# Cluster attention and a gated FFT convolution on one core: the last batch's products may run on GpSimd, two x1 blocks go through ScalarE, and the whole order is new

## The chip, the cores and the metric

The kernel runs on one core of a Trainium2 chip. The metric is device time in microseconds: the median of the runs of one program. A core has TensorE (PE, matmul), VectorE (DVE), ScalarE (ACT), GpSimd (POOL) and SyncE (SP, which issues DMAs here). Each engine takes its instructions in program order, so an instruction that waits holds up everything behind it on its engine.

## The reference

Inputs are q, k and v of shape 4 x 8 x 768 x 64 and 16 centroids per head. Each query and each key is given the nearest centroid of its head by cosine; a query attends only to keys with the same centroid:

```python
q_assign = np.argmax(np.einsum('bhsd,hcd->bhsc', q_n, c_n), axis=-1)
k_assign = np.argmax(np.einsum('bhsd,hcd->bhsc', k_n, c_n), axis=-1)
mask = q_assign[:, :, :, None] == k_assign[:, :, None, :]
scores = np.where(mask, scale * np.matmul(q, k.transpose(0, 1, 3, 2)), -1000000000.0)
attn = softmax(scores);  x = matmul(attn, v)          # heads joined: 4 x 768 x 512
```

The result x feeds a gated convolution along the sequence:

```python
proj = x @ w_proj;  x1, x2, x3 = proj[..., :D], proj[..., D:2*D], proj[..., 2*D:]
x2_conv = np.fft.irfft(np.fft.rfft(x2, axis=1) * np.fft.rfft(filter_fft, axis=0), axis=1)
out = (x1 * x2_conv * x3) @ w_out
```

## The kernel before, in words

The work is a list of small operations that a planner inside the kernel sets in order. For every operation there is an engine or a choice of engines with a cost for each, a due time, the data it reads and writes, and the PSUM banks it takes and gives back. The planner gives every engine the operation that can start first, and among nearly equal ones the one that is due first. `NUDGE` is a table that moves the due time of each numbered operation, and `ONLY` is a table that ties an operation to one engine. What comes out is one fixed order for each engine. The order is not decided on the chip.

There are eight groups of four heads (two groups make one batch), each in two halves of two heads. For a half, the scores are made in 18 PSUM banks (lines 82 and 84: scores, two 64-column matmuls for each product, or one of 128 columns), ScalarE takes the exponentials (L694, L697), TensorE multiplies by v (L708), and VectorE adds up the exponentials for the denominators (L725, L729). The routing of the next group lies between: transposes of q and k (L594, L607), copies into `qkP` and casts into `aug` (L282 on ScalarE, L284 on VectorE or GpSimd, one helper), similarities (L512, L627), the largest of each (L529 to L536, L638 to L642), masks (`ohT`, L653, L655) and DMAs of them into `aug`.

When two groups are done, the function `hyena(b)` does the convolution of their batch. It is spread over the attention of the next batch, except for the last batch, where nothing else is left to lie beside it. Its steps are these:

- U (L843): x2 in six PSUM banks. For the last batch, the part of four of them that needs the last heads (`kt` = 3) is a matmul of its own. Sums and differences follow (L857, L862) into `uv2`.
- The spectrum (L84, L475), its products with the filter's spectrum (L873, VectorE, two for each of six banks), and their sums into `y` (L877, VectorE or GpSimd).
- G, 16 banks (L84 on `xT`, `wpj`): for each of four blocks of 128 channels (`dt`) and each half of the sequence (`ch`), x3 and x1. x3 is copied out (L282 or L284); then VectorE multiplies x1, straight from PSUM, into that copy (L917, the gate). In the last batch the copies lie in `qkP`, which the routing no longer needs.
- The inverse transform, two banks for each `dt` (L84 or L82 on `inv`, `y`). One is copied to `od` (or `rb`), sum and difference go into `sd` (L944) for `dt` 0 and 1, and a fold makes the values in their order, in `yy` for even `dt` and `sim` for odd (L954). For `dt` 2 and 3 of the last batch the fold reads PSUM itself.
- The product with the gate into `y2` (L959): in the last batch two of 384 columns for each `dt`, on VectorE.
- W (L84 on `wout`, `y2`): six blocks of 128 rows of the output, copied out of PSUM and written by DMA (L982, L1001, L1005).

VectorE and GpSimd operations that are marked `lock` get an order between them: a GpSimd one waits until the last such VectorE one that stands before it in the program is done.

For x1 before the change (line 916):

```python
                    else:
                        op(("DVE", .55), lambda e, ch=ch, x3=x3, h=h: T.nc.vector.tensor_tensor(
                            x3()[:, ch], ap(h)[:, :384], x3()[:, ch], op=Alu.mult), due + .8,
                           r=[h], w=xkeys[ch], free=[h])
```

Of the kernel before, what the change touches and what calls it, by code (L numbers as in the profile page):

```python
# [19 lines left out]
Alu = mybir.AluOpType  # L20
# [66 lines left out]
class Plan:  # L87
# [6 lines left out]
    def op(self, eng, fn, due, r=(), w=(), alloc=None, free=(), lock=False, byts=0, after=(), kind=None, lat=0.0, tab=None):  # L94
        o = Op()
        o.eng = eng if isinstance(eng, dict) else {eng[0]: eng[1]}
        o.fn, o.due, o.alloc, o.free, o.lock, o.byts, o.kind = fn, due, alloc, free, lock, byts, kind
        o.seq = len(self.ops)
        o.due += NUDGE.get(o.seq, 0.0)
        o.outs, o.end, o.start, o.on = [], None, None, None  # L100
        deps, o.soft = set(after), set(after)
        o.lat, o.tab = lat, tab
        for key in r:
            deps.update(self.writers.get(key, ()))
        for key in w:
            deps.update(self.writers.get(key, ()))
            deps.update(self.reads.get(key, ()))
        for key in r:
            self.reads.setdefault(key, []).append(o)
        for key in w:  # L110
            self.writers[key] = [o]
            self.reads[key] = []
        deps.discard(o)
        o.deps = deps
        o.left = len(deps)
        for d in deps:
            d.outs.append(o)
        for h in free:
            h.readers += 1
        self.ops.append(o)  # L120
        return o
# [143 lines left out]
def build(T):  # L265

    P = Plan()
    op = P.op
# [11 lines left out]
    def copy(e, out, in_):  # L280
        if e == "ACT":
            T.nc.scalar.copy(out, in_)  # L282
        else:
            (T.nc.vector if e == "DVE" else T.nc.gpsimd).tensor_copy(out, in_)  # L284
# [3 lines left out]
    def ap(h):  # L288
        return bank(h.ids[0])
# [16 lines left out]
    def alu(e):  # L306
        return T.nc.vector if e == "DVE" else T.nc.gpsimd

    EV384 = {"ACT": .465, "DVE": .55}
# [507 lines left out]
    def hyena(b):  # L817
        xs = b % 2
        last = b == B - 1
# [12 lines left out]
        for m in range(3):  # L832
            pair_ = ((2, 3), (5, 4), (0, 1))[m]
            tb = m % 2
            for w_ in range(2):
                h = Bank()
                due = step(.87)
# [21 lines left out]
            if m == 2:  # L859
                for e_ in range(2):  # L860
                    for g_, o_ in ((0, Alu.add), (1, Alu.subtract)):
                        op({"DVE": .68, "POOL": 1.5}, lambda e, e_=e_, g_=g_, o_=o_: alu(e).tensor_tensor(  # L862
                            T.uv2[:, e_, g_], T.tm[0][:, 1 - e_], T.tm[1][:, 1 - e_], op=o_), due + 1.4 + .1 * e_,
                           r=[("tm", x, 1 - e_) for x in range(2)] + [("tm", x) for x in range(2)], w=[("uv2", e_, g_)], lock=True)
        for i in range(3):
            for cs in range(2):
                h = Bank()
                due = step(.44)
                op(("PE", .432), lambda e, i=i, cs=cs, h=h: spectrum4(ap(h), i, cs), due,
                   r=[("uv2", e_, m) for e_ in ((i,) if i < 2 else (0, 1)) for m in (e_ ^ cs, 2)] + [("fw", m, cs) for m in range(2)],  # L870
                   w=[h], alloc=h, kind="proj" if i < 2 else "half")
# [4 lines left out]
            for r in range(2):  # L876
                op({"POOL": 1.5, "DVE": .68}, lambda e, i=i, r=r: alu(e).tensor_tensor(  # L877
                    T.y[:, i, r], T.tm[r][:, 0], T.tm[r][:, 1], op=Alu.add if r else Alu.subtract), due + 2, r=[("tm", r, 0), ("tm", r, 1)],
                   w=[("y", i, r)], lock=True)
# [4 lines left out]
        for dt in range(ND):  # L884
# [13 lines left out]
            for ch in range(2):  # L898
                for off in (2 * DM, 0):
                    h = Bank()  # L900
                    due = step(.66)
                    if last:
                        due = w1 - 8 + 5 * ch + dt

                    def G(e, dt=dt, ch=ch, off=off, h=h):
                        for kt in range(ND):
                            x = T.xT[xs][:, kt, ts(ch, 384)].rearrange("p (t n) -> p t n", n=128)
                            columns(ap(h)[:, :384].rearrange("p (t n) -> p t n", n=128), T.wpj[:, kt, off + dt * 128:off + dt * 128 + 128],
                                    x[:, :, ::-1] if ch else x, kt == 0, kt == ND - 1)
                    g = op(("PE", .648), G, due, r=XT + WPJ, w=[h], alloc=h, kind="proj",  # L910
                           after=[] if last else gs[-1:] + (inv[dt - 2:dt - 1] if dt > 1 else []))
                    gs.append(g)
                    if off:
                        op(EV384, lambda e, ch=ch, x3=x3, h=h: copy(e, x3()[:, ch], ap(h)[:, :384]), due + .8,
                           r=[h], w=xkeys[ch], free=[h])
                    else:
                        op(("DVE", .55), lambda e, ch=ch, x3=x3, h=h: T.nc.vector.tensor_tensor(  # L917
                            x3()[:, ch], ap(h)[:, :384], x3()[:, ch], op=Alu.mult), due + .8,
                           r=[h], w=xkeys[ch], free=[h])
# [37 lines left out]
            for ch in range(2) if last else [slice(0, 2)]:  # L957
                cols = slice(384 * ch, 384 * ch + 384) if last else slice(0, S)
                op(("DVE", .55) if last else {"DVE": .95, "POOL": 2.1}, lambda e, dt=dt, ch=ch, cols=cols, x3=x3, yy=yy: alu(e).tensor_tensor(  # L959
                    T.y2[:, dt, cols], yy().rearrange("p t c -> p (t c)")[:, cols],  # L960
                    x3()[:, ch] if last else x3().rearrange("p a b -> p (a b)"), op=Alu.mult), due + 2.5,
                   r=ykeys[ch::2] + xkeys[ch] if last else ykeys + xkeys[0] + xkeys[1],
                   w=[("y2", dt, ch)] if last else [("y2", dt, 0), ("y2", dt, 1)], lock=True)
# [320 lines left out]
```

## Time and profile before

| what | value |
|---|---|
| runs | 372.38, 370.62, 372.59 us; median 372.38 us |
| the profiled execution's own time | 370.64 us |
| its span, first to last instruction | 368.9 us |
| TensorE busy | 357.5 us, 97% of the span |
| VectorE busy | 342.5 us, 93% |
| ScalarE busy | 263.6 us, 71% |
| GpSimd busy | 120.9 us, 33% |
| HBM traffic over the span | 106 GB/s on average |
| granted TensorE clock | 1.00 |

Busy time of an engine is the time in which one of its instructions runs. The chain that ended last is followed back from the last instruction, at each step to what released it. A group's row gives the line, the engine, what is written and read, the number of instructions, their busy time together and the mean time of one in ns; instructions of one engine overlap a little, so busy time can be less than number times mean.

### The profile page before, as it was taken

The page shows a single profiled execution, that of the slowest core. Times are in us where ns is not written, and L with a number is a line of the kernel's source. Part 1 is how long each engine was busy: PE and PEld are TensorE (multiplying, and loading weights), DVE is VectorE, ACT ScalarE, POOL GpSimd, SP SyncE. Part 2 cuts the span into 40 slices and gives each one's busy share as a digit, 9 for nine tenths or more (in the row PEclk, how much of TensorE's full clock was granted, in tenths as well). Part 3 has the DMA queues.
Part 4 walks back from the last instruction along what each step waited for, and adds up shares of the span by engine and source line. Part 5 has one row for each costly group of instructions (what it writes and reads, how often), then busy time and mean ns, then how long its engine had stood idle before and what let it go on. Part 6 is the DMA issues. An engine that isn't in the chain of part 4 may idle for free.

```text
span 368.9 us, 8653 instructions
## 1 busy us (share of the span) xinstructions
PE 357.5 (97%) x3314; PEld 208.9 (57%) x3316; DVE 342.5 (93%) x478; ACT 263.6 (71%) x495; POOL 120.9 (33%) x162
## 2 busy tenths in 40 slices
PE   7899999999999999999999999999999999999985
PEld 4455544555856565565555555566555655566672
DVE  7999999896999899999999999998998999999994
ACT  7998978877986859769869765899584785433242
POOL 7730730422032752331530044352221334016610
PEclk9999999999999999999999999999999999999999
DMA  7986597484247768748556964667477750110124
GB/s 175 202 189 126 128 211 195 93 189 110 62 80 156 115 156 169 152 103 129 107 64 183 238 170 81 146 152 98 81 116 167 150 77 1 48 45 2 59 115 171
DMA packets 90405, 46.20 MB, mean 125 GB/s; under 512 B 78248, under 2 KB 84092, under 8 KB 90364
## 3 DMA queue, kind: packets, MB, share of 16 engines
q1 hardware_dynamic: 85500, 36.15, 40.5%
q0 software_dynamic: 2752, 8.98, 17.1%
q10 hardware_dynamic: 2112, 0.52, 0.6%
q8 instruction: 26, 0.43, 0.5%
q14 instruction: 15, 0.12, 0.1%
HBM read 31.59 MB, written 7.40 MB: 106 GB/s over the span
## 4 chain that ended last, share of the span: by engine, by line
PE 78%; DVE 11%; ACT 5%; issue 3%; DMA 1%; POOL 1%; SPq 0%; DVEq 0%; ACTq 0%; POOLq 0%
PE bank L84 33%; PE pair L708 28%; PE bank L843 5%; PE bank L594 5%; DVE acc L729 3%; PE bank L627 2%; ACT p L697 1%; PE bank L82 1%; DMA qkraw<-in_k_dram 1%; DVE qkP L284 1%; PE bank L475 1%; PE bank L742 1%; ACT p L694 1%; PE bank L607 1%; DVE ohT L655 1%
## 5 line engine op out<-in xcount | busy, mean ns | idle before, releaser
L708 PE MATMUL pair<-p,vraw 128*64 128x385 f32 x768 | 143.0, 489 | 0.1
L697 ACT ACTIVATE p<-bank 128x512 f32<-128x512 f32 x192 | 108.7, 606 | 23.5 <-PE bank L84 16.0
L729 DVE TENSOR_TENSOR acc<-p,acc 128x1536 f32<-128x1536 f32 x64 | 112.8, 1762 | 3.2 <-ACT p L694 0.5
L84 PE MATMUL bank<-aug,aug 80*64 80x512 bf16 (+3 forms) x736 | 81.9, 327 | 2.1 <-ACT p L697 0.9
L708 PEld LDWEIGHTS pair<-p,vraw 128*64 128x64 f32 x768 | 56.6, 136 | 43.8 <-issue 36.7
L84 PEld LDWEIGHTS <-aug 80*64 80x64 bf16 (+1 forms) x736 | 45.6, 109 | 41.0 <-issue 26.3
L694 ACT ACTIVATE p<-bank 128x512 f32<-128x512 f32 x96 | 57.4, 606 | 5.4 <-PE bank L84 3.6
L284 POOL CAST aug<-qkP 64x768 bf16<-64x768 f32 x29 | 25.9, 900 | 83.3 <-DVE acc L729 55.9
L762 POOL DMA_DIRECT2D acc<-acc x30 | 24.4, 824 | 69.8 <-DMA acc<-acc 37.4
L84 PE MATMUL bank<-xT,wpj 128*64 128x384 bf16 x504 | 47.2, 326 | 0.0
L84 PEld LDWEIGHTS <-wpj 128*64 128x64 bf16 x504 | 30.2, 110 | 14.1 <-issue 2.6
L282 ACT COPY qkP<-bank 128x512 f32<-128x512 f32 (+1 forms) x46 | 23.1, 559 | 15.9 <-PE bank L594 9.7
L84 PEld LDWEIGHTS <-y 128*64 128x64 bf16 x472 | 24.0, 110 | 13.2 <-issue 3.6
L725 POOL TENSOR_TENSOR acc<-p,p 128x512 f32<-128x512 f32 x15 | 19.3, 1297 | 32.3 <-DVE acc L729 10.4
L873 DVE TENSOR_TENSOR tm<-bank,hm 128x512 f32<-128x512 f32 x44 | 28.1, 681 | 1.9 <-POOL uv L862 0.8
L84 PE MATMUL bank<-wout,y 128*64 128x512 bf16 (+1 forms) x200 | 24.0, 371 | 1.1 <-DVE y L959 1.1
L282 ACT CAST aug<-qkP 64x768 bf16<-64x768 f32 x28 | 23.2, 830 | 1.0 <-DVE qkP L284 0.4
L843 PE MATMUL bank<-wpj,xT 128*64 128x512 bf16 x192 | 22.7, 379 | 0.4 <-ACT p L697 0.4
L725 DVE TENSOR_TENSOR acc<-p,p 128x512 f32<-128x512 f32 x33 | 21.6, 690 | 0.4 <-DMA dd<-acc 0.4
L877 POOL TENSOR_TENSOR y<-tm 128x512 bf16<-128x512 f32 x14 | 17.8, 1277 | 12.8 <-DVE tm L873 10.6
L732 ACT COPY osb<-pair 128x770 f32<-128x770 f32 x16 | 12.9, 806 | 10.8 <-PE pair L708 10.7
L594 PEld LDWEIGHTS bank<-ident,qkraw 128*128 128x128 f32 x144 | 15.6, 141 | 6.3 <-ACT p L694 2.4
(178 smaller groups left out, 435.7 us busy)
## 6 DMA issues: line engine op xcount, KB each, us to landing
vraw<-in_v_dram SPq DMA_DIRECT2D x16, 384.0 KB, 5.2
qkraw<-in_q_dram SPq DMA_DIRECT2D x30, 192.0 KB, 3.9
rb<-dr SPq DMA_DIRECT2D x30, 192.0 KB, 3.7
qkraw<-in_k_dram SPq DMA_DIRECT2D x28, 192.0 KB, 3.6
out_dram<-ob SPq DMA_DIRECT2D x9, 512.0 KB, 5.0
acc<-acc POOLq DMA_DIRECT2D x10, 384.0 KB, 4.8
acc<-acc POOLq DMA_DIRECT2D x10, 192.0 KB, 4.2
y<-in_moe_filter_fft_dram SPq DMA_DIRECT2D x4, 384.0 KB, 4.3
```

Source lines behind the costliest of these rows:

```text
L84: T.nc.tensor.matmul(out[64 * i:64 * i + 64], lhsT[:, 64 * i:64 * i + 64], rhs, start=start, stop=stop)
L282: T.nc.scalar.copy(out, in_)
L284: (T.nc.vector if e == "DVE" else T.nc.gpsimd).tensor_copy(out, in_)
L594: T.nc.tensor.transpose(bank(h.ids[i // 4])[:, ts(i % 4, 128)], raw(ss[i // NT], i % NT), T.ident[:, ::-1] if 3 <= i < NT else T.ident)
L694: T.nc.scalar.activation(o, ap(h).rearrange("p (a b) -> p a b", a=2), Act.Exp, scale=0.125)
L697: T.nc.scalar.activation(flat(s)[:, lo:lo + 512], ap(h), Act.Exp, scale=0.125)
L708: T.nc.tensor.matmul(o[64 * hp:64 * hp + 64, ch, :385], T.vraw[vs][:, hp, sk * D:(sk + 1) * D], T.p[slots[sk]][:, hp, 384 * ch:384 * ch + ...
L725: alu(e).tensor_tensor(o, x, y, op=Alu.add)
L729: T.nc.vector.tensor_tensor(T.acc[os], T.p[slots[sk]][:, :, :S], T.acc[os], op=Alu.add)
L762: op(("POOL", .8), lambda e, rows=rows: T.nc.gpsimd.dma_start(flat_()[:rows], flat_()[rows:2 * rows], accum_op=Alu.add), te, r=[], w=AK, b ...
L843: T.nc.tensor.matmul(ap(h)[64 * i:64 * i + 64], T.xT[xs][:, kt, c:c + 64], T.wpj[:, kt, DM:2 * DM], start=kt == 0, stop=kt == ND - 1)
L873: op(("DVE", .68), lambda e, i=i, cs=cs, r=r, h=h: T.nc.vector.tensor_tensor(T.tm[r][:, cs], ap(h), hmrow(i, (0, 2, 2, 3)[2 * r + cs]), op ...
```

## The change

1. For the last batch and `dt` 0 and 1, x1 is no longer multiplied straight from PSUM. It is copied out (ScalarE or VectorE) into `T.x3[dt]`, a buffer that the last batch did not use, and the product of the two copies may run on VectorE or on GpSimd.
2. The eight products into `y2` of the last batch may run on VectorE or on GpSimd. (The fold of `dt` 0 and 1 already could.)
3. `NUDGE` and `ONLY` are new throughout. So the order of every engine is new from the first instruction on, and some operations of all stages change their engine.

```diff
-NUDGE = {0:-244.575,1:-2716.133,2:-17.613,3:-10.463,
...
+NUDGE = {0:-656.35,1:-5800.852,2:-34.602,3:28.863,
...
+                    elif last and dt < 2:
+                        op(EV384, lambda e, ch=ch, dt=dt, h=h: copy(e, T.x3[dt][:, ch], ap(h)[:, :384]), due + .8,
+                           r=[h], w=[("x3", dt, ch)], free=[h])
+                        op({"DVE": .55, "POOL": 1.1}, lambda e, ch=ch, dt=dt, x3=x3: alu(e).tensor_tensor(
+                            x3()[:, ch], T.x3[dt][:, ch], x3()[:, ch], op=Alu.mult), due + 1.4,
+                           r=[("x3", dt, ch)], w=xkeys[ch], lock=True)
                     else:
...
-                op(("DVE", .55) if last else {"DVE": .95, "POOL": 2.1}, lambda e, dt=dt, ch=ch, cols=cols, x3=x3, yy=yy: alu(e).tensor_tensor(
+                op({"DVE": .55, "POOL": 1.1} if last else {"DVE": .95, "POOL": 2.1}, lambda e, dt=dt, ch=ch, cols=cols, x3=x3, yy=yy: alu(e).tensor_tensor(
                     T.y2[:, dt, cols], yy().rearrange("p t c -> p (t c)")[:, cols],
                     x3()[:, ch] if last else x3().rearrange("p a b -> p (a b)"), op=Alu.mult), due + 2.5,
```

In the changed program, lines behind 915 have moved down by six; the text keeps the numbers of the program before unless it says otherwise.

More of the change, by code (lines that the diff above doesn't have):

```diff
@@ L43 @@
-ONLY = {13:"POOL",14:"POOL",15:"POOL",16:"POOL",18:"POOL",30:"ACT",32:"SP",33:"SP",36:"SP",37:"SP",40:"ACT",41:"DVE",66:"ACT",69:"DVE",72:"POOL",73:"ACT",85:"DVE",86:"DVE",93:"DVE",94:"POOL",97:"DVE",99:"DVE",100:"DVE",101:"POOL",141:"DVE",153:"DVE",213:"ACT",226:"POOL",227:"POOL",233:"POOL",238:"POOL",244:"POOL",245:"DVE",253:"DVE",254:"ACT",257:"DVE",288:"DVE",357:"POOL",358:"DVE",359:"POOL",394:"ACT",404:"ACT",406:"DVE",407:"DVE",408:"POOL",409:"ACT",416:"POOL",417:"POOL",418:"POOL",427:"DVE",430:"ACT",461:"POOL",462:"DVE",463:"DVE",498:"DVE",525:"POOL",533:"POOL",549:"DVE",551:"ACT",555:"ACT",566:"DVE",589:"DVE",593:"POOL",594:"POOL",600:"DVE",604:"DVE",639:"DVE",691:"POOL",692:"ACT",693:"POOL",694:"POOL",696:"ACT",697:"ACT",698:"ACT",699:"POOL",700:"POOL",701:"DVE",711:"DVE",808:"POOL",809:"POOL",856:"DVE",858:"ACT",859:"ACT",861:"POOL",862:"POOL",867:"POOL",913:"DVE",915:"POOL",1002:"DVE",1005:"DVE",1018:"DVE",1067:"ACT",1070:"DVE",1072:"ACT",1075:"ACT",1077:"DVE",1146:"POOL",1147:"POOL",1152:"DVE",1153:"DVE",1154:"POOL",1156:"ACT",1164:"ACT",1168:"ACT",1201:"DVE",1313:"DVE",1315:"ACT",1369:"DVE",1416:"ACT",1421:"ACT",1426:"ACT",1448:"DVE",1457:"DVE",1516:"POOL",1600:"POOL",1601:"POOL",1607:"POOL",1608:"POOL",1609:"POOL",1610:"DVE",1621:"DVE",1812:"ACT",1875:"DVE",1886:"DVE",1919:"ACT",1920:"SP",1922:"DVE",1923:"SP",1926:"SP",1930:"SP",1933:"ACT",1934:"SP",1938:"SP",1942:"SP"}
@@ new lines @@
+ONLY = {14:"POOL",15:"POOL",16:"POOL",18:"POOL",29:"SP",30:"ACT",32:"SP",36:"SP",38:"SP",39:"ACT",40:"ACT",44:"DVE",50:"DVE",65:"DVE",72:"ACT",89:"DVE",93:"DVE",94:"POOL",100:"POOL",101:"POOL",143:"DVE",147:"DVE",149:"ACT",155:"DVE",176:"DVE",177:"POOL",178:"DVE",226:"POOL",227:"POOL",232:"DVE",233:"POOL",238:"POOL",239:"POOL",244:"POOL",253:"ACT",254:"DVE",405:"ACT",407:"DVE",408:"POOL",409:"DVE",410:"ACT",413:"ACT",415:"ACT",416:"ACT",417:"POOL",418:"POOL",429:"DVE",461:"DVE",463:"DVE",498:"ACT",508:"DVE",522:"POOL",524:"DVE",525:"DVE",532:"POOL",548:"DVE",559:"DVE",564:"DVE",570:"ACT",577:"DVE",592:"DVE",600:"DVE",604:"ACT",688:"ACT",689:"ACT",690:"ACT",692:"POOL",693:"ACT",694:"ACT",696:"ACT",699:"POOL",700:"ACT",701:"ACT",857:"DVE",858:"DVE",859:"DVE",861:"DVE",862:"ACT",869:"POOL",870:"ACT",879:"DVE",914:"POOL",915:"POOL",1031:"DVE",1032:"DVE",1047:"DVE",1054:"DVE",1061:"POOL",1067:"DVE",1072:"ACT",1094:"DVE",1095:"POOL",1147:"POOL",1153:"ACT",1154:"DVE",1155:"ACT",1156:"ACT",1164:"ACT",1165:"DVE",1167:"ACT",1168:"DVE",1199:"DVE",1314:"POOL",1315:"ACT",1368:"POOL",1369:"POOL",1416:"DVE",1421:"ACT",1426:"ACT",1448:"DVE",1486:"DVE",1487:"DVE",1501:"DVE",1504:"DVE",1515:"POOL",1526:"DVE",1607:"ACT",1608:"POOL",1622:"DVE",1767:"DVE",1768:"DVE",1819:"ACT",1825:"ACT",1862:"DVE",1864:"DVE",1867:"DVE",1879:"ACT",1880:"POOL",1885:"POOL",1893:"DVE",1924:"SP",1927:"SP",1929:"DVE",1930:"SP",1933:"ACT",1934:"SP",1938:"SP",1945:"ACT"}
```

2 lines of the change are left out of this document (1 added, 1 removed).

## The prediction

> **What bounds the kernel now.** First I read the busy shares, then TensorE's waits, then the stretches of the end, then the rows of the operations that the change touches.
>
> ```profile
> PE 357.5 (97%) x3314; PEld 208.9 (57%) x3316; DVE 342.5 (93%) x478; ACT 263.6 (71%) x495; POOL 120.9 (33%) x162
> ```
>
> TensorE works for 357.5 of 368.9 us, so only its 11.4 us of idle time can be won, as long as its own work stays the same. VectorE, at 93%, is the only other engine near its limit. The view of who waited for whom, for TensorE alone, says where the idle time lies:
>
> ```profile
> PE bank L1096 <- DVE wpj L1100: 1.1, 1, 1.1
> PE bank L84 <- DVE y L959: 1.1, 1, 1.1
> PE bank L607 <- DMA qkraw<-in_k_dram: 0.9, 1, 0.9
> PE bank L84 <- ACT p L697: 0.9, 3, 0.5
> PE bank L512 <- DVE qkP L284: 0.7, 1, 0.7
> PE bank L84 <- DVE ohT L655: 0.7, 1, 0.7
> ```
>
> Columns: total, times, longest. Three of these lie in the start (L1096, L607, L512: 2.7 us), one in the tail (L959: 1.1 us), the others in the attention. Then the stretches (length, and busy time with number of instructions for PE, PEld, DVE, ACT, POOL):
>
> ```profile
> 326.49:333.89 7.40, 7.40 (x85) 4.87 (x87) 7.03 (x15) 2.44 (x6) 3.46 (x2) 1.00 0.02 4
> 341.41:355.00 13.59, 13.59 (x182) 9.35 (x180) 13.34 (x25) 4.27 (x9) 6.32 (x5) 1.00 0.19 78
> 355.00:362.43 7.43, 6.36 (x97) 4.34 (x92) 7.43 (x17) 2.67 (x6) 1.00 (x1) 1.00 0.18 73
> 362.43:364.64 2.21, 2.20 (x20) 0.93 (x18) 0.34 (x2) 1.58 (x4) 0.00 (x0) 1.00 0.76 276
> 364.64:368.93 4.29, 0.00 (x0) 0.00 (x0) 0.69 (x1) 0.00 (x0) 0.00 (x0) 1.00 0.59 224
> ```
>
> 326.49 is the last denominator matmul (L742), 341.41 the last sum into `uv2`, 362.43 the end of the last `y2` product, 364.64 the last matmul. The reader is to see that in the tail both engines are full. TensorE has 36.7 us of work from L742 on (38.15 less 1.44 idle); VectorE is 100% busy from 355 to 362.43, and there TensorE waits 1.07 us for its products. After the last matmul come 4.29 us of copy and DMA. The rows:
>
> ```profile
> L917 DVE TENSOR_TENSOR qkP<-bank,qkP 128x384 f32<-128x384 f32 x8 | 4.2, 551 | 0.1
> L954 POOL TENSOR_TENSOR yy<-sd 128x384 f32<-128x384 f32 x6 | 6.0, 1014 | 4.6 <-DVE acc L729 3.1 <-DVE yy L954 1.2 <-DVE sd L944 0.2
> L959 POOL TENSOR_TENSOR y<-yy,x 128x768 bf16<-128x768 f32 x5 | 9.2, 1839 | 17.1 <-DVE yy L954 13.8 <-DVE xT L808 3.2
> L282 ACT COPY x<-bank 128x384 f32<-128x384 f32 x19 | 9.0, 481 | 4.5 <-PE bank L84 4.5
> ```
>
> **The change part by part.** Which engine got what, I take from the order in which the two programs' instructions stand.
>
> TensorE's work is the same. One full-width inverse transform (8 matmuls, 0.82 us) has become 16 of half width (0.83 us); a few score products changed the other way. In both programs there are 63 places where the next matmul has another width. So what counts is idle time, and the sum has four terms: start, attention, tail, output.
>
> *Whole engines.* VectorE loses 8 instructions, by the rows 4.0 us. ScalarE gains 11.3 us: seven casts into `aug` (7 x 0.83 = 5.8), six copies into `x` (2.9), the rest small. GpSimd loses nine casts (8.1 us), gains five products at about 1.0, and comes out 5.5 us lower.
>
> *Tail, VectorE.* From the first L857 to the last `y2` VectorE had 4 x 0.684 + 1.23 before the sums into `uv2`, then 4 sums (2.74), 12 spectrum products (8.17), 8 gates (4.4), one `y` (0.69), 4 `sd` (2.2), 7 folds (3.85) and 8 `y2` products (4.4): 31.8 us by the rows' means; 28.5 by the clock, since instructions overlap by some 0.07. Now it has 6 L857 (4.1), 4 sums, 12 products, 4 old gates (2.2) and 2 new ones (1.1), one `y`, 4 `sd`, 8 folds (4.4), 5 `y2` (2.75) and two copies that ScalarE used to do (1.24): 29.6. So 2.2 us less. The other two gates and three `y2` products (all of the first sequence half, `dt` 0 to 2) are GpSimd's. A price for these is not in the trace: half of the 1839 ns product is 0.92, the 1014 ns fold has the shape; I take 1.0 (bounds 0.92 and 1.27, the row of L877 with 512 columns). The four x1 copies cost ScalarE 4 x 0.48, in a tail where it is busy for a third; if it were not free, each would hold a bank and a gate up by 0.48.
>
> *Tail, TensorE.* I followed the new order by these durations, with t = 0 at the first U matmul with `kt` = 3. The sums into `uv2` end at 7.7, the `y` sums at 17.6, and TensorE reaches the inverse of `dt` 0 at 18.6 without a wait. `dt` 3's inverse comes behind a W block (0.87), ends at 24.75, and ScalarE has copied it to `rb` at 25.3; VectorE, through with its other work at 24.6, waits 0.7 for it. Its fold and product end at 26.4. GpSimd's three products end at 22.5, 24.0 and 25.05, earlier than that. The W block of the first 128 rows needs all four and waits from 25.4 to 26.4: 1.0 us. The last `y2` is done at 29.8; behind it are only last parts of W, 0.7 to 1.4 us. The last matmul ends at 31.2, of which 1.2 idle, against 1.44 before: **-0.2 us**. Ends: -1.4 (no idle left) and +2.0 (three GpSimd products, up to 1.0 each, of which 1.0 is under the wait that is there anyway). So VectorE's 2.2 us are not won: the `rb` copy is late next, and TensorE had only 1.07 to give.
>
> *Output.* At 363.55 before, 1.1 us ahead of the last matmul, the last four pieces of 256 KB were started; 1.0 MB then flowed at some 380 GB/s. In the new order four of the six blocks still leave at the end, the first of them 0.65 us ahead of the last matmul, since VectorE copies it behind its last product. That is 0.45 later; the last piece is smaller (128 KB). **+0.35**; ends 0 and +0.9.
>
> *Start.* VectorE is full from 5 to 20 us (4.6 to 4.9 of each 5), and its mask chain sets the first score. Before that score it now has one more turn (0.41) and one more mirror (0.56) of the angles and a cast (0.54), and one copy (0.55) and one mask row (0.55) less: **+0.4**. Ends -0.3 (the mask row now goes through ScalarE beside the others, 0.55, and GpSimd's early memsets cost nothing) and +1.0 (the similarity matmuls move too, since `identb` and `identr`, 0.35 and 0.67, now stand between the `qkP` copies).
>
> *Attention.* The 0.7 us wait for L655 at 33 us: before, L655 stood behind three L725 and two L729 (1.76 each) on VectorE; now behind one L725, so its banks come free some 3.5 us sooner and the scores no longer wait. **-0.7**. The other waits (1.8 us) I leave as they are; each belongs to its place in the order and may go or come again. Ends: -2.5 (all gone) and +2.5 (twice as many). Mask DMAs on SP move ahead with L655; a load behind them moves by their 0.6 us issues, and the only load that TensorE waited for is the one in the start.
>
> **Sum:** +0.4 - 0.7 - 0.2 + 0.35 = -0.15 us. The profiled execution took 370.64, the median is 372.38, and the executions lie in two pairs (370.62 and 370.64; 372.38 and 372.59), of which I know no cause. I lay the sum on the mean of the four, 371.56: **371.4 us**.
>
> **The rivals.**
>
> *Faster: the waits go.* With VectorE 4.0 us lighter, the attention's 2.5 us and the tail's 1.07 go for the most part: 371.56 - 3 = 368.6. For it: the waits for VectorE are the largest. Against: those for ScalarE (0.9) get no relief, as ScalarE has 11.3 us more.
>
> *Slower: the shared port.* GpSimd's products lie among VectorE operations that read two SBUF operands (folds from `sd`, the new gates, `y2`). If one blocks the other, VectorE's last stretch grows by up to 3 x 1.0 us, and from t = 24.6 on nothing is spare: every microsecond beyond the 1.0 us wait is one of the end. With the two gates as well up to 4 us: 375 at most, 374.4 as the case. For it: at 11.27 us two GpSimd memsets beside a VectorE cast took 0.47 and 0.45 us, 0.09 a moment earlier. Against: the `lock` order keeps such pairs apart, and in the tail before, VectorE waited for GpSimd only 0.3 us.
> The Trainium skill, "SBUF — State Buffer", section "SBUF: two separate sides", says that VectorE with two SBUF inputs and a GpSimd operation that reads SBUF take the shared port pair from each other for a whole instruction; by that rule this rival would hold for each pair that meets, the forecast if the order keeps them from meeting. The memsets agree that one holds up the other.
>
> *Slower: ScalarE's casts.* Seven more casts of 0.83 us stand among the exponentials, and each can hold a score bank. If half of them do: 3.5 x 0.83 = 2.9, and 374.4. For it: TensorE waits for L697 already. Against: ScalarE is 71% busy, and TensorE has six other banks.
>
> *The change does less than it says.* That is in the forecast: GpSimd does run five products, yet VectorE's relief is hidden behind TensorE.
>
> **How the numbers follow.** The runs of one program differ by 0.5%, and so 0.5% is about what can be told from no change: 370.5 and 374.2 are the bounds. Forecast, within 0.5%: 0.40. Waits gone: 0.36. Shared port: 0.13. ScalarE's casts: 0.11. So faster 0.36, same 0.40, slower 0.24. The range goes from 368.4 (the faster case) to 375.0 (the port at its most); the forecast's own range is 370.5 to 373.
>
> **What would show it.** Right: the first score near 22.9 us; no wait for L655 near 33; in the tail one TensorE wait of about 1.0 for the `y2` product of `dt` 3, VectorE waiting for ScalarE's `rb`, and 4.5 us after the last matmul. Wrong: GpSimd products well above 1.0 us or VectorE folds waiting for them; more than 1 us of waits for ScalarE in the attention; a first score after 23.5; TensorE busy time other than 357.5.

## The result and the profile after

The changed kernel takes 375.15 us (median of six runs, 373.98 to 376.86), the kernel before 370.64 us (median of six runs, 370.49 to 372.59). The ratio is 1.0105 with a 95% interval of 1.0071 to 1.0140: slower by 1.05%, where 371.4 us and no measurable change were forecast. The profiled execution of the changed kernel took 374.32 us; its span is 372.6 us against 368.9, so 3.7 us are to be found in the trace.

The busy shares of the changed kernel:

```profile
PE 360.2 (97%) x3327; PEld 216.4 (58%) x3327; DVE 340.9 (91%) x470; ACT 273.6 (73%) x512; POOL 114.9 (31%) x157
```

VectorE lost eight instructions and ScalarE gained ten microseconds, as the order said, and yet TensorE is busy for 2.7 us more. TensorE's idle time by what ended it (total, times, longest; the larger ones):

```profile
PE bank L594 <- DMA qkraw<-in_q_dram: 1.2, 1, 1.2
PE bank L1102 <- DVE wpj L1106: 1.1, 1, 1.1
PE bank L84 <- ACT p L697: 1.1, 2, 0.7
PE bank L512 <- DVE qkP L284: 1.1, 1, 1.1
PE bank L84 <- DVE y L965: 0.6, 1, 0.6
PE bank L607 <- DMA qkraw<-in_k_dram: 0.4, 1, 0.4
PE bank L84 <- POOL y L965: 0.4, 1, 0.4
```

The wait for L655 at 33 us is gone, as forecast. The first line is new: a load of q, in the middle of the attention. The two waits for L965 (the y2 products) add up to what was one wait before. But TensorE's idle time grew by 1.0 us only (12.4 instead of 11.4), because a matmul that is held up by its weight load can count as busy: the view of the weight loads shows waits where the matmuls show none. The same view for the weight loads of the tail, from 320 us on:

```profile
PEld L84 <- DVE y L965: 1.8, 3, 0.9
PEld L84 <- POOL y L965: 0.8, 1, 0.8
```

Before, the same weight loads waited for `y2` for 2.0 us, now for 2.6. So I also worked out, from the starts of all matmuls, how long each block of equal matmuls took beyond its number times the lower quartile of the pitch of that shape (the pitch is the time from one matmul's start to the next; one for each shape, taken over the kernels of this study). This takes in the hidden waits:

| stretch of the span | before | after | after, profiled again |
|---|---|---|---|
| 0 to 60 us | 8.24 | 9.01 | 9.15 |
| 60 to 160 | 4.71 | 4.33 | 4.33 |
| 160 to 220 | 1.07 | 2.67 | 2.52 |
| 220 to 320 | 3.19 | 3.34 | 3.32 |
| 320 to the last matmul | 1.85 | 2.78 | 2.79 |
| the matmuls at their own pace | 345.57 | 345.89 | 345.89 |
| behind the last matmul | 4.29 | 4.58 | 4.6 |

The sums are the spans, 368.9, 372.6 and 372.6. One thing is to be allowed for: the trace of the kernel before lacks the records of two full-width matmuls between 60 and 160 us (it has 3314 matmuls for 3316 weight loads, and three profiles of the same order have two more there). They are worth 0.43 us, which the table books before as lost time instead of as work. So the stretch from 60 to 160 us lost and won next to nothing, and TensorE's own work did not grow. Three places lost: the start, the stretch from 160 to 220, and the end.

**The start.** TensorE's first matmul of a score starts at 23.08 us instead of 22.49, 0.59 later, near the forecast. But the first exponential starts 1.04 us later, and TensorE waits for it. ScalarE of the changed kernel:

```profile
21.63 0.80 ACT L555 ACTIVATE aug<-bank 16x768 bf16<-16x768 bf16 x1
22.45 1.28 ACT L408 ACT_TABLE_LOAD   x1
23.74 0.20 ACT L408 ACTIVATE warm<-half_pi 128x1 f32<-128x1 f32 x1
23.97 1.08 ACT L697 ACTIVATE p<-bank 128x512 f32<-128x512 f32 x2
```

Before, ScalarE loaded the table of the exponential at 21.02, while VectorE made all the mask rows. Now one mask row and one more copy into `qkP` go through ScalarE, and the table load stands behind them. The size varies with the execution: over all profiles of this study the first exponential starts at 22.92 to 23.25 us with the old start and at 23.96 to 24.11 with the new one, 0.9 later in the mean.

**The end.** The stretches that answer to those shown of before (329.64 is the last denominator matmul, 338.22 the first L857, 344.54 the last sum into `uv2`, 366.46 the end of the last y2 product, 368.02 the last matmul):

```profile
329.64:338.22 8.58, 8.58 (x100) 4.96 (x100) 8.41 (x17) 2.52 (x5) 1.02 (x1) 1.00 0.01 2
338.22:344.54 6.32, 6.32 (x71) 4.73 (x69) 6.25 (x11) 3.43 (x7) 2.84 (x2) 1.00 0.02 4
344.54:355.00 10.46, 10.46 (x119) 6.42 (x116) 10.13 (x19) 3.13 (x7) 7.31 (x6) 1.00 0.13 52
355.00:366.46 11.46, 10.42 (x156) 6.92 (x152) 10.47 (x22) 4.93 (x10) 3.96 (x4) 1.00 0.33 128
366.46:368.02 1.56, 1.55 (x22) 1.02 (x20) 1.30 (x3) 0.66 (x2) 0.00 (x0) 1.00 0.27 102
368.02:372.60 4.58, 0.00 (x0) 0.00 (x0) 0.00 (x0) 0.57 (x2) 0.00 (x0) 0.76 0.60 222
```

From the first L857 to the last `y2` VectorE needs 28.24 us, against 28.54 before: of the 2.2 us that it was to be spared, 0.3 are left. It is busy for 1.3 us less there, and it idles for 1.0 us of the 11.46 from 355 on, where it had no gap before. And it starts late: the first L857 stands 8.58 us behind the last denominator matmul instead of 7.40. The GpSimd products are as forecast:

```profile
L919 POOL TENSOR_TENSOR qkP<-x,qkP 128x384 f32<-128x384 f32 x2 | 2.0, 1006 | 5.4 <-ACT qkP L282 3.3 <-ACT x L282 2.1
L965 POOL TENSOR_TENSOR y<-yy,qkP 128x384 bf16<-128x384 f32 x2 | 2.0, 997 | 1.6 <-DVE yy L960 1.6
```

### The profile page after: what moved, and what is told of

It is laid out like the page before. It is cut to its first block, busy times and chain, and to the rows that moved or that the text cites. A ratio compares the mean times of both kernels' runs of the same rounds, so it can differ in the third digit from the quotient of the medians.

```text
span 372.6 us, 8647 instructions
## 1 busy us (share of the span) xinstructions
PE 360.2 (97%) x3327; PEld 216.4 (58%) x3327; DVE 340.9 (91%) x470; ACT 273.6 (73%) x512; POOL 114.9 (31%) x157
## 4 chain that ended last, share of the span: by engine, by line
PE 70%; ACT 11%; DVE 10%; issue 4%; DMA 3%; SPq 1%; ACTq 1%; DVEq 0%
PE bank L84 30%; PE pair L708 25%; PE bank L843 5%; ACT p L697 4%; PE bank L594 3%; DVE acc L729 3%; ACT p L694 2%; DMA qkraw<-in_q_dram 2%; ACT aug L282 1%; PE bank L627 1%; DVE acc L725 1%; PE bank L742 1%; DMA aug<-ohT 1%; PE bank L607 1%; PE bank L512 1%
## 5 line engine op out<-in xcount | busy, mean ns | idle before, releaser
L697 ACT ACTIVATE p<-bank 128x512 f32<-128x512 f32 x192 | 108.5, 608 | 16.9 <-PE bank L84 11.6
L729 DVE TENSOR_TENSOR acc<-p,acc 128x1536 f32<-128x1536 f32 x64 | 113.1, 1767 | 3.1 <-ACT p L697 0.8
L84 PE MATMUL bank<-aug,aug 80*64 80x512 bf16 (+3 forms) x742 | 84.4, 327 | 1.7 <-ACT p L697 1.1
L708 PEld LDWEIGHTS pair<-p,vraw 128*64 128x64 f32 x768 | 59.7, 136 | 39.9 <-issue 33.1
L84 PEld LDWEIGHTS <-aug 128*64 128x64 bf16 (+1 forms) x742 | 48.0, 109 | 38.8 <-issue 26.6
L84 PE MATMUL bank<-xT,wpj 128*64 128x384 bf16 x504 | 48.1, 326 | 0.4 <-DVE tm L857 0.4
L284 POOL CAST aug<-qkP 64x768 bf16<-64x768 f32 x20 | 19.3, 965 | 68.3 <-DVE acc L729 19.7
L84 PEld LDWEIGHTS <-wpj 128*64 128x64 bf16 x504 | 32.4, 110 | 13.4 <-issue 4.1
L282 ACT COPY qkP<-bank 128x512 f32<-128x512 f32 (+1 forms) x48 | 24.5, 554 | 15.1 <-PE bank L594 9.8
L84 PEld LDWEIGHTS <-y 128*64 128x64 bf16 x488 | 24.5, 110 | 14.1 <-issue 4.2
L282 ACT CAST aug<-qkP 64x768 bf16<-64x768 f32 x35 | 28.8, 830 | 1.8 <-PE bank L84 1.0
L84 PE MATMUL bank<-wout,y 128*64 128x512 bf16 (+1 forms) x200 | 24.2, 371 | 1.0 <-DVE y L965 0.6
L725 DVE TENSOR_TENSOR acc<-p,p 128x512 f32<-128x512 f32 x34 | 24.5, 740 | 0.6 <-ACT p L697 0.5
L725 POOL TENSOR_TENSOR acc<-p,p 128x512 f32<-128x512 f32 x14 | 17.9, 1302 | 19.5 <-DVE acc L725 11.2
L877 POOL TENSOR_TENSOR y<-tm 128x512 bf16<-128x512 f32 x15 | 18.9, 1274 | 13.8 <-DVE tm L873 8.3
L594 PEld LDWEIGHTS bank<-ident,qkraw 128*128 128x128 f32 x144 | 15.6, 141 | 7.7 <-ACT p L697 3.6
```

The costliest lines, as they stand in the source:

```text
L84: T.nc.tensor.matmul(out[64 * i:64 * i + 64], lhsT[:, 64 * i:64 * i + 64], rhs, start=start, stop=stop)
L594: T.nc.tensor.transpose(bank(h.ids[i // 4])[:, ts(i % 4, 128)], raw(ss[i // NT], i % NT), T.ident[:, ::-1] if 3 <= i < NT else T.ident)
L697: T.nc.scalar.activation(flat(s)[:, lo:lo + 512], ap(h), Act.Exp, scale=0.125)
L708: T.nc.tensor.matmul(o[64 * hp:64 * hp + 64, ch, :385], T.vraw[vs][:, hp, sk * D:(sk + 1) * D], T.p[slots[sk]][:, hp, 384 * ch:384 * ch + ...
L725: alu(e).tensor_tensor(o, x, y, op=Alu.add)
L729: T.nc.vector.tensor_tensor(T.acc[os], T.p[slots[sk]][:, :, :S], T.acc[os], op=Alu.add)
```

## The experiments

In all but the plain repeat the planner's own choice is replaced by a list that names the operations in order, with their engines and banks; the list is that of one of the two kernels with the change shown. Because of the list, lines of these kernels lie 52 (L82 to about L190) or 95 further down than in the kernel they are made from: L84 is L136, L594 is L689, L742 is L837. The letters of the theories: A, the loss is a sum of separate waits made by the new order; B, the GpSimd products; C, ScalarE's casts; D, formed on the first results, the new order leaves the transfers thin margins.

### Which part of the change costs the time

The new order up to 322 us of its plan, then the operations and order of before:

```diff
 order of the changed kernel, operations planned before 322 us
-order of the changed kernel, the rest
+order of the kernel before, the rest, with its operations
```

> The new order up to the last heads' scores, then the old tail: old order, gates straight from PSUM on VectorE, all products into y2 on VectorE. Theory A: tail and output give 0.7 and 0.3 back, about 374.1. Theory B: nearly all of the 4.5 us come back, 371.5 or less. Theory C: no change, 375.1.

Measured: 375.31 us (373.84 to 376.95), ratio 1.0121 (1.0084 to 1.0157). Without a single one of the new operations the time stays where it was. B as the whole cause is out. The profiled run of this kernel was the longest of its four (376.95), and up to 322 us its order is the one of the changed kernel. So it shows what such a long run waits for:

```profile
PE bank L689 <- ACT p L789: 1.2, 1, 1.2
...
PE bank L938 <- DVE xT L903: 1.0, 1, 1.0
```

The profile of the changed kernel has neither. The first stands at 120 us, ahead of transposes of q. The view names an exponential that had long ended; by the trace's records of completions, the q load issued at 112.13 us was complete at 121.08, and the transposes began at 121.17. In the changed kernel the same load was complete at 119.81 for a start at 119.92. The second follows from VectorE, which stood still for 2.51 us until the transfer `dd<-acc` was done, at 206.25. Both are transfers that came late.

The reverse, the order of before and then the new tail:

```diff
 order of the kernel before, operations planned before 322 us
-order of the kernel before, the rest
+order of the changed kernel, the rest, with its operations
```

> The other way round: the old order up to the last heads' scores, then the new tail with its copies and GpSimd's products. Theory A: 0.7 and 0.3 more than the kernel before, about 371.6. Theory B: 374 or more. Theory C: as before, 370.6.

Measured: 373.13 us (372.43 to 374.38), ratio 1.0062 (1.0042 to 1.0083). No theory had this: the new tail costs more than the 1 us of A. Behind 318 us this trace is 1.6 us of TensorE time and 0.5 us of output longer than that of before. The two hybrids don't add up to the whole (their seams are new orders too), so they only say that both parts cost. And 374.38, the run that was profiled, is the longest of the five.

The new operations in the order of before:

```diff
 order of the kernel before
+x1 of dt 0 and 1: copies on ScalarE, where the gates stood
-gates of dt 1, y2 of dt 0, 1 and 2 (first half) on VectorE
+gates of dt 1, y2 of dt 0, 1 and 2 (first half) on GpSimd
```

> The order of the kernel before, with the new operations alone: x1 of dt 0 and 1 copied out by ScalarE, their gates and the y2 products on the engines that the changed kernel gives them (GpSimd: two gates, three y2 products). Theory A (the operations are harmless, the new order costs the time): VectorE loses about 2.75 us in the tail and the 1.07 us wait for y2 shrinks, 370.0 (369.5 to 370.9). Theory B (the GpSimd products hold VectorE up): 372.5 or more, with VectorE folds and products beside them longer than 0.55 us.

Measured: 371.54 us (ten runs, 371.27 to 371.85), ratio 1.0018 (1.0008 to 1.0027). Neither theory: the operations alone cost 0.7 us, although VectorE has less to do. The timeline of its tail shows where the relief went:

```profile
352.55 0.88 ACT L377 COPY x<-bank 128x384 f32<-128x384 f32 x2
353.30 0.52 ACT L377 COPY od<-bank 128x384 f32<-128x384 f32 x1
...
353.85 1.02 DVE L1045 TENSOR_TENSOR sd<-bank,od 128x384 f32<-128x384 f32 x2 [1.09 <-ACT od L377]
360.68 1.08 DVE L1060 TENSOR_TENSOR y<-sim,qkP 128x384 bf16<-128x384 f32 x1
362.26 1.06 DVE L1060 TENSOR_TENSOR y<-sim,qkP 128x384 bf16<-128x384 f32 x1
...
360.35 1.00 POOL L1060 TENSOR_TENSOR y<-sim,qkP 128x384 bf16<-128x384 f32 x1 [1.85 <-DVE sim L1055]
361.90 1.00 POOL L1060 TENSOR_TENSOR y<-yy,qkP 128x384 bf16<-128x384 f32 x1 [0.56 <-DVE y L1060]
```

Two x1 copies on ScalarE stand ahead of the `od` copy, and VectorE waits 1.09 us for it. And twice a VectorE product of two SBUF operands takes 1.07 us instead of 0.55: it began 0.3 us behind a GpSimd product and ended 0.4 us behind its end. The Trainium skill, "SBUF — State Buffer", section "SBUF: two separate sides", has it that the one that starts first keeps the shared ports for its whole instruction; these two agree with that. In the changed kernel every VectorE operation that lies beside a GpSimd product by more than 0.1 us reads PSUM (or is a copy from it), and all of those keep their 0.55 or 0.68 us. So this rival has a mechanism, but the new order keeps clear of it.

The other way round, the new order with its five GpSimd products on VectorE:

```diff
 order of the changed kernel
-gates of dt 1, y2 of dt 0, 1 and 2 (first half) on GpSimd
+gates of dt 1, y2 of dt 0, 1 and 2 (first half) on VectorE
```

> The changed kernel's order, with its five GpSimd products put on VectorE at their places in the list. Theory A: 5 x 0.47 us come back on VectorE in the last 15 us, where TensorE waits for y2 already: +1.5 to +2.5, 376.6 to 377.6. Theory B (GpSimd products cost more than they spare): 373 or less.

Measured: 376.92 us (375.52 to 377.32), ratio 1.0152 (1.0123 to 1.0182), as A had it. TensorE's wait for `y2`, 1.0 us with GpSimd's help, is:

```profile
PE bank L136 <- DVE y L1060: 2.1, 3, 1.1
```

So within the new order GpSimd's products gain 1.8 us by the medians (375.15 with them; the two kernels' runs overlap a little) and 1.45 us by the traces, from the last denominator matmuls to the last matmul (38.38 against 39.83 us). They are not the loss.

### The transfers

The q load for which TensorE waited, and its k half, issued ahead of two loads of the next group instead of behind those, eight mask DMAs and a v load:

```diff
 SyncE, 144 to 160 us of the plan:
+qkraw<-in_q (half), qkraw<-in_k (half)
 qkraw<-in_k x2 (of the next group)
 aug<-ohT x8, dr<-dn, rb<-dr x2, vraw<-in_v, dd<-acc
-qkraw<-in_q (half), qkraw<-in_k (half)
```

> The changed kernel with two of its DMAs moved: the loads of the q and k halves that TensorE waited for at 169.6 us stand ahead of the next group's two loads, of eight mask DMAs and of a v load on SyncE, not behind them. Theory A (the loss is a sum of separate waits that the new order made: start 0.5, this load 1.2 to 1.5, tail 0.7, output 0.3): the wait of 1.2 us for in_q goes and the time falls by 1.2 to 1.5, to about 373.8. Theory B (GpSimd's products hold VectorE up in the tail) and theory C (the casts that ScalarE got hold the exponentials up all through the attention): no change, 375.1.

Measured: 374.05 us (373.24 to 374.51), ratio 1.0083 (1.0060 to 1.0106): 1.1 us less than the changed kernel, near A's 373.8, and the wait is gone. But the interval overlaps that of the changed kernel, the profiled spans differ by 0.7 us only (371.9 and 372.6), and a later kernel that moves this pair and five more loads took 374.75. So that the wait went is shown, and what it was worth is not. SyncE's queue in the changed kernel shows where the load stood:

```profile
157.44 2.52 SPq L497 DMA_DIRECT2D aug<-ohT  x4
160.06 1.17 SPq L779 DMA_DIRECT2D rb<-dr  x2
161.28 1.22 SPq L497 DMA_DIRECT2D aug<-ohT  x2
162.60 0.53 SPq L328 DMA_DIRECT2D vraw<-in_v_dram  x1
163.31 0.32 SPq L766 DMA_DIRECT2D dd<-acc  x1
163.69 0.62 SPq L323 DMA_DIRECT2D qkraw<-in_q_dram  x1
```

By the order's plan its buffer had been free for 22 us. TensorE wanted the data at 169.59 and got them at 170.79, 7.1 us after the issue. The plan reckons 4.4 us for this load; in the trace the loads of q and k whose landing the profile tells take 2.5 to 7.2. The trace also records sixteen completions for each load: fifteen of this one's had come by 167.78, as planned, and the last came at 170.66. So most of the lateness is one late part of the transfer and not the place in the queue.

The first 24 us in the order of before, the rest as changed:

```diff
-order of the changed kernel, operations planned before 24 us
+order of the kernel before, operations planned before 24 us
 order of the changed kernel, the rest
```

> The changed kernel, but all that the old plan starts in its first 24 us comes in the old plan's order and on its engines; the rest in the new order. Theory A: the first exponential comes 1.0 us sooner (23.4 for 24.4), and the end 0.5 to 1.0 sooner, about 374.4. Theories B and C: no change at the end, 375.1.

Measured: 375.05 us (374.02 to 375.57), ratio 1.0117 (1.0093 to 1.0141). The first exponential stood 0.9 us earlier, and by the median the end did not (the interval would leave room for a part of it). In this profile TensorE doesn't wait at 169 us, but 0.9 us for a mask DMA at 195.5. Another 0.27 us went in the tail, where the wait for `y2` at 362 us is 0.91 instead of 0.64; it is so in both kernels with the old start, and no transfer stands behind it. The terms of A didn't add, and hence theory D. Its first test is the changed kernel itself, profiled once more.

> The changed kernel itself, profiled a second time. Theory D (the new order leaves the transfers thin margins, so that TensorE's waits for what a DMA brings fall in other places from one execution to the next): the waits that no DMA stands behind come again at the same places to 0.1 us (start, 361 to 363 us), but the 1.20 us for the q load at 169.6 us is gone, smaller or joined by another of 0.4 us or more between 60 and 330 us; median 374.0 to 376. Theory A (a fixed sum of separate waits): the same list of waits, 169.6 us with 1.2 among them; median 375.1.

Measured: 374.65 us (four runs, 373.76 to 375.07), and from 160 to 222 us:

```profile
PE bank L84 <- DMA aug<-ohT: 0.4, 1, 0.4
PE bank L594 <- DMA qkraw<-in_k_dram: 0.2, 1, 0.2
```

D holds. The q load was issued at the same place (163.89 instead of 163.69 us), but its last completion came at 169.56 instead of 170.66. The same program waits 0.16 us at 170.6 instead of 1.20 at 169.6, and 0.37 for a mask at 195.5 instead of nothing; the sum of the stretch is nearly the same (2.52 against 2.67 in the table), and behind 9 us all waits of 0.4 us or more that no DMA stands behind come again, as long as before to 0.02 us.

Seven loads of q and k moved ahead, all that the new order plans less than 6 us before their use:

```diff
 SyncE, each load moved to where its buffer is free:
-qkraw at 73, 77, 112, 160, 160, 183 and 217 us of the plan
+qkraw at 65, 73, 86, 144, 144, 150 and 168 us of the plan
```

> The changed kernel with seven loads of q and k halves moved ahead on SyncE's queue, to where their buffers are free: those that the new order issues 4.4 to 5.7 us (by the order's own plan) ahead of their first use, at 73, 77, 112, 160, 160, 183 and 217 us; afterwards 9 us or more. Theory D (transfers with thin margins): no wait of TensorE for qkraw after 20 us, median 373.6 to 374.2 (the early pair alone gave 374.05), and the runs lie closer together than 373.8 to 376.9. Rival (the one pair was all there was to win, or other transfers on SyncE are late instead): 374.0 to 375.2, with new waits for masks or rb.

Measured: 374.75 us (five runs, 374.28 to 376.36), ratio 1.0105 (1.0087 to 1.0123): the rival. No wait for `qkraw` is left behind 20 us, but at 195 us there is this one:

```profile
PE bank L136 <- DMA aug<-ohT: 0.8, 1, 0.8
```

With the old start as well:

```diff
-order of the changed kernel, operations planned before 24 us
+order of the kernel before, operations planned before 24 us
 order of the changed kernel with the seven loads ahead
```

> The same, with the first 24 us in the order of the kernel before. The old start alone gave nothing (375.05), although its first score stood 0.9 us earlier: waits later took it. Theory D (that was taken by waits for transfers at 195 us and behind): with the loads ahead the 0.9 us reach the end, 372.8 to 373.3. Rival (something else gives the start's gain back, so the terms don't add): the same time as new_order_loads_ahead to 0.4 us.

Measured: 373.43 us (372.79 to 374.41), ratio 1.0065 (1.0051 to 1.0079): 1.3 us less than with the loads alone. Once no load is late, the gain of the start does reach the end (0.1 us beside the forecast of D, far from the rival), although TensorE still waits 1.1 us for the mask at 194.8. So what is late next is the mask DMAs on the same queue. They are eight issues in a row, and these took 6.09 us in the changed kernel and 7.52 in its second profile:

```profile
188.83 7.52 SPq L497 DMA_DIRECT2D aug<-ohT  x8
```

The order of before has such places too. The experiment with the new tail repeats it to 318 us, and in its profile, unlike that of before, TensorE waits 1.54 us at 67.5 us for the denominators. Its SyncE, VectorE and TensorE:

```profile
50.95 3.68 SPq L423 DMA_DIRECT2D vraw<-in_v_dram  x1
66.17 1.02 DVE L903 SCALAR_TENSOR_TENSOR xT<-osb,rb 128x768 bf16<-128x768 f32 x1 [1.93 <-DMA rb<-dr]
69.00 0.85 PE L837 MATMUL bank<-acc,ones 128*32 128x384 f32 x8 [1.54 <-DVE acc L824]
```

The v load before it was issued in 2.73 us in the profile of before, here in 3.68; so `dr` and `rb` followed 0.9 us later, VectorE stood still for `rb` (1.93 us, of which the late issue explains half), and the L729 behind it came late for the denominator matmul. The run of this profile is 1.2 to 1.95 us above the other four of its kernel, and the first six runs of before lie at 370.5 to 370.7 and at 372.4 to 372.6 (its later runs lie between as well): 1.54 is near that distance. That it is the same wait was not shown, since no upper run of before was profiled.

### Single steps of the forecast, in the order of before

L655 ahead of the second L729, the step of -0.7:

```diff
 VectorE, 27 to 33 us:
 L729
-L729
 L655 x2
+L729
 L729
```

> The kernel before with one operation moved: the second L729 stands behind the two L655 on VectorE instead of ahead of them, as the new order has it. My step of -0.7: the wait of 0.66 us at 33 us goes and the end comes that much sooner, 370.1. Rival: the sums that now stand later hold the exponentials' buffers, a wait of the same size follows within 30 us, and the time stays 370.7.

Measured: 371.63 us (ten runs, 371.53 to 372.29), ratio 1.0025 (1.0015 to 1.0034). The rival holds, and worse: the wait at 33 us is gone, but the two L655 wait 0.29 and 0.26 us for TensorE and ScalarE, the sums behind them are late, and TensorE waits for those at 37.3:

```profile
PE bank L837 <- DVE acc L824: 1.4, 1, 1.4
...
31.18 0.55 DVE L750 TENSOR_SCALAR ohT<-bank 64x384 bf16<-64x384 f32 x1 [0.29 <-PE bank L136]
31.99 0.56 DVE L750 TENSOR_SCALAR ohT<-bank 64x384 bf16<-64x384 f32 x1 [0.26 <-ACT ohT L748]
32.59 3.55 DVE L824 TENSOR_TENSOR acc<-p,acc 128x1536 f32<-128x1536 f32 x2
```

One `y2` product on GpSimd, with nothing else moved:

```diff
-y2 of dt 0, first half, on VectorE
+y2 of dt 0, first half, on GpSimd, beside sd<-bank,rb
```

> The kernel before with one operation moved to GpSimd: the y2 product of dt 0 for the first half of the sequence, placed beside VectorE operations that read PSUM (the sums into sd from rb). No x1 copies, the rest of the order as before. Theory A (VectorE's 7.43 us without a gap before the last matmuls set the end, and a GpSimd product costs it nothing when the VectorE operation beside it reads PSUM): VectorE loses 0.47 us there, the wait of 1.07 us falls to 0.6, 370.3 against 370.75. Rival (ScalarE's rb copy is late next, since the sums then want it sooner): no gain, 370.7 to 370.9, and VectorE waits 0.3 to 0.5 us for rb.

Measured: 371.29 us (twelve runs, 370.68 to 372.85), ratio 1.0015 (1.0002 to 1.0029). No gain, and above the rival's 370.9 too; the rival's wait is there, and TensorE still waits 1.06 us:

```profile
356.37 1.02 DVE L1039 TENSOR_TENSOR sd<-bank,rb 128x384 f32<-128x384 f32 x2 [0.36 <-ACT rb L377]
```

The same with the `rb` copy made sooner:

```diff
 TensorE
+inverse of dt 1
 W block of batch 2
-inverse of dt 1
 ScalarE
+rb<-bank
 ob<-bank
-rb<-bank
 VectorE
-y2 of dt 0, second half
 sd<-bank,rb x2
+y2 of dt 0, second half
```

> The kernel before with the same y2 product on GpSimd, and the rb copy made sooner: on TensorE the inverse of dt 1 stands ahead of the last W block of batch 2 instead of behind it, on ScalarE the rb copy ahead of that block's ob copy, and on VectorE the two sums from rb ahead of the y2 product left of dt 0. Theory A (with one product alone, VectorE's relief of 0.47 us was lost to the late rb copy, 0.36 us of waiting): now VectorE waits less than 0.1 us for rb, the wait of TensorE before the last W blocks falls from 1.07 to about 0.6, and the kernel takes 370.3 to 370.5, less than both. Rival (the wait moves on once more, to the next copy or to the y2 rows that W still reads): the wait of TensorE stays at 1.0, and 370.8 or more.

Measured: 370.90 us (twelve runs, 370.50 to 372.36), ratio 0.9997 (0.9981 to 1.0013): the same as before, as the rival had it. VectorE doesn't wait for `rb` any more, but the tail, from the last denominator matmul to the last matmul, is shorter by 0.13 us only (37.71 against 37.84):

```profile
PE bank L136 <- DVE y L1054: 1.0, 1, 1.0
...
355.41 1.02 DVE L1039 TENSOR_TENSOR sd<-bank,rb 128x384 f32<-128x384 f32 x2
356.35 0.55 DVE L1054 TENSOR_TENSOR y<-yy,qkP 128x384 bf16<-128x384 f32 x1
356.94 1.02 DVE L1049 TENSOR_TENSOR yy<-bank,od 128x384 f32<-128x384 f32 x2
```

Of the 0.47 us, 0.13 are a gap ahead of 355.41 (the fold ended at 355.28), 0.04 one ahead of 356.94, and the rest goes because operations no longer overlap by 0.08 us at these seams. Nothing tried here beats the kernel before.

## Why the prediction was wrong, step by step

The forecast was a sum of four terms that nearly cancelled, -0.15 us, laid on 371.56. The 3.7 us of the profile, by the same terms (with the two missing matmuls counted):

| term | forecast | measured | where it is from |
|---|---|---|---|
| start | +0.4 | +1.0 | first exponential at 23.97 instead of 22.93 |
| attention | -0.7 | +1.5 | the table: 0 to 60 us without the start -0.27, then +0.05, +1.60, +0.15 |
| tail | -0.2 | +0.9 | the table, from 320 us |
| output | +0.35 | +0.3 | 4.58 us instead of 4.29 |
| TensorE's own work | 0 | -0.1 | the table |

- **Start: right in kind, at the upper end of its range.** The first score came 0.59 us later (0.4 forecast). What failed is "the mask row now goes through ScalarE beside the others", put down as a possible gain of 0.3: ScalarE was the last to be ready, since its table load of 1.28 us stands between the mask row and the first exponential. The runs with the old start bear out the size (1.3 us with the loads ahead).
- **Attention: the step that decided.** That the wait for L655 goes was right. That the 0.7 us are then won was not shown for the new order, and in the old order they came back as a wait of 1.36 us. In the changed kernel VectorE is early for L655 and stands still 1.78 us for TensorE ahead of it, at 30.18. "The only load that TensorE waited for is the one in the start" was true of that one execution; how little time the others had to spare was not worked out. The new order plans seven q or k loads less than 6 us ahead of their use behind the start, the old one three, and the loads take up to 7.2 and more. The range of this term, 2.5 us either way, did hold the result.
- **Tail: the cause named was right, the size was not.** That "the `rb` copy is late next" is seen in the changed kernel (0.49 us of VectorE's idle time), and alone in the run with one product. Three things were missed. TensorE's idle time in the tail before was 1.07 us and not 1.44, so there was less to win. The walk through the tail began at the first U matmul with VectorE nearly free for L857, whereas it had four operations of batch 2 left, 2.3 us, behind the last `xT`. And it counted only TensorE's idle time: its weight loads' waits for `y2` grew from 2.0 to 2.6 us. The printed terms of VectorE's old tail add up to 30.4 us; the 31.8 holds with six L857 for the four written there, as the trace has them.
- **Output and TensorE's own work: right.** So were the price of a GpSimd product (1.0 us) and that GpSimd would not hold VectorE up in this order. The 360.2 us of TensorE's busy time, one of the signs of being wrong, come from held-up matmuls that count as busy.
- **The base: too high.** 371.56 was the mean of two pairs; all later runs of the kernel before have their median at 370.6 to 371.0.
- **The range: not the sum of its parts.** The upper ends of the four terms make +6.4 us together, yet the range stopped at 375.0, the price of the port rival; 375.15 lies just above it. Slower had a chance of 0.24, all of it for two rivals that were not the cause.

Of the rivals, the port is real but avoided (old order: twice 0.5 us; new order: none). The memsets named for it stand beside a cast with one SBUF operand and are no such pair. ScalarE's casts did not do it: TensorE's waits for L697 went from 0.9 to 1.1 us, and the one behind the table load alone grew by 0.4. ScalarE got most of its new work between 60 and 160 us (3.6 us) and between 220 and 320 (4.5 us), and there TensorE lost 0.05 and 0.15. No run put the casts back. "The waits go" failed because a wait is a place in an order and not a stock that shrinks with VectorE's load: VectorE is 1.6 us less busy, and the kernel slower.

The profiled loss is thus placed, but not all of it is explained: in the trace with the early loads the stretch from 160 to 220 us is still some 0.9 us above that of before, and no run took the tail's loss away. The medians differ by 4.5 us, 0.8 more than the profiles. The profiled executions of the changed kernel (374.32 and 374.31) are near the lower end of its runs; the one long run of this order that was profiled, with the old tail, waited for a q load, for `dd` and for a mask. Open, too, is why one order's masks at 195 us are late more often than the other's: a mask landed at 194.32 for a score at 194.40 before, and at 197.55 for one at 197.59 after, so both have no margin there, and the trials moved loads, not masks.

## What to carry to other kernels

When an order is new throughout, list for every transfer how long before its use it is issued, beside the slowest landing of its kind in the trace; the ones without margin are where waits come up, now at one and now at another, and a wait removed in one place can be handed to the next of them. Relief on an engine counts only up to the next copy that this engine waits for, so follow the copies of the helper engine (here ScalarE's `od`, `rb` and the table load) before booking it. And count the waits of the weight loads with TensorE's idle time: here they were most of the tail's loss.

## What the runs showed of the hardware

- SyncE needs 0.58 us (median) to issue a DMA, but in every profile some issues take more than 1 us: 20 of 238 in the kernel before (up to 2.85), 19 to 25 in the other profiles of its order (up to 5.00), 20 to 27 of 236 or 237 in those of the new order (up to 5.85). They are not the same ones each time: the first of the eight mask DMAs near 189 us took 0.64 us in one execution of the changed kernel and 2.09 in the other. What stands behind on the queue is late by that much. Why was not tried.
- One part of a transfer can be late alone. Of the sixteen completions of the q load at 163.7 us, fifteen came within 4.1 us of the issue and the last after 7.0; in the second execution, within 3.95 and after 5.7. Why was not tried.
- A VectorE product of two SBUF operands beside a GpSimd product took 1.06 and 1.08 us instead of 0.55, while 0.55 and 0.68 us operations with an operand in PSUM kept their time beside the same products.
- A gain of 0.9 us at the start of a kernel whose TensorE is 97% busy need not reach the end: in the profile with the old start, TensorE then waited 0.9 us for a mask at 195.5 us and 0.27 us more in the tail.
